# Starting a fused attention and feed-forward kernel on Trainium2: E and F over two queues and cast early, k ahead of half of q, and the q repack moved

## The chip, the cores and the metric

The kernel runs on one core of one Trainium2 chip. The metric is the device time of one execution in microseconds (us). An execution takes about 415 us, and executions of one kernel mostly agree within 0.3% (here four of the kernel before lie from 414.90 to 415.64 us). One of several executions is profiled. The engines are named here as in the profile: PE is TensorE (matmul), PEld its weight loads, DVE is VectorE, ACT is ScalarE, POOL is GpSimd, and SP is SyncE, which here only issues transfers. PSUM is the memory that PE writes its results to; another engine copies them out.

## The reference, cut to what matters

Attention over a projected sequence (E and F shorten k and v from 1024 to 64 rows), followed by a feed-forward layer that takes the maximum of three up-projections:

```python
# q, k, v: (8, 8, 1024, 64); E, F: (64, 1024)
k_proj = np.einsum('ks,bhsd->bhkd', E, k)
v_proj = np.einsum('ks,bhsd->bhkd', F, v)
attn   = softmax(q @ k_proj.transpose(0, 1, 3, 2) / 8)
x      = (attn @ v_proj).transpose(0, 2, 1, 3).reshape(8192, 512)
h      = np.maximum(np.maximum(x @ w1, x @ w2), x @ w3)   # 512 -> 768
out    = h @ w_out                                        # 768 -> 512
```

## The kernel before

The batches are pipelined: while the feed-forward layer of one batch runs, the attention of the next is fitted between its steps. Batch 0 has nothing to hide behind, so its start is a series of small dependent steps. It loads, casts and transposes E, F and q, projects k, computes the scores of its four head pairs (numbered 0 to 3), and projects v. In the names below, T means transposed: kp and vp are k and v projected, kpT is kp transposed, xT is the attention's result, and hT what the down-projections read. `idle(n)` issues n filler matmuls on a constant tile, whose results nobody reads.

```python
def idle(n):
    t, ns = bank()
    for _ in range(n):
        nc.tensor.matmul(out=t, lhsT=warm[:, 0:P], rhs=warm, start=True, stop=True)
    free[ns[0]] = pe(n * MM)

nc.scalar.dma_start(out=ef_f[0:KP], in_=E)          # ScalarE's queue
nc.scalar.dma_start(out=ef_f[KP:P], in_=F)          # behind E
for i in range(2):                                  # SP's queue: q, q, k, k, v
    nc.sync.dma_start(out=q_f[i], in_=view(q, 0)[:, 4 * i:4 * i + 4, 0:SPC])
for i in range(2):
    nc.sync.dma_start(out=k_f[i], in_=view(k, 0)[:, 4 * i:4 * i + 4])
for (a, b), t in zip(v_heads, v_f):
    nc.sync.dma_start(out=t, in_=view(v, 0)[:, a:b])
# ... (cut)
idle(9)
cast_q(0, "v"); cast_q(1, "s")        # "v" VectorE, "s" ScalarE, "g" GpSimd
turn_ef()                             # 8 fp32 transposes on PE, 2 copies
turn_q(0); turn_q(1)
idle(3)
cast_q(2, "v"); cast_q(3, "s")
turn_q(2); turn_q(3)
idle(7)
cast_k(0, 0, "v"); cast_k(0, 1, "s")
kp = k_half(0)                        # first k projection
# ... (cut: scores, exps, second k projection, sums, casts of v)
idle(3)
v_part(0)                             # first v projection
copy("v", v_t[:, 4:6], v_f[1])
for g in (2, 3):
    invert(0, g, *C0, sums(0, g, *C0))
scale_x(0, 0, *C0, values(0, 0, *C0))
idle(2)
copy("v", v_t[:, 6:8], v_f[2])
v_part(1)
scale_x(0, 1, *C0, values(0, 1, *C0))
idle(2)
v_part(2)
scale_x(0, 2, *C0, values(0, 2, *C0))
# then the first up-projection of the feed-forward layer
```

For later batches q is repacked by four VectorE copies and turned by a DMA transpose. The plan says behind which step this stands: steps 0 to 5 are up-projections, 6 to 9 down-projections.

```python
out = {(0, 1): [za(n, 0), sc(n, 1)], (0, 3): [za(n, 1), sc(n, 2)], ...}   # cut
if n + 1 < B:
    out[0, 4] = [qd(n + 1)]           # the repack of q
```

The softmax here doesn't subtract the row's maximum and nothing guards it: scores larger than these inputs give would overflow.

Of the kernel before, what the change touches and what calls it, by code (L numbers as in the profile page):

```python
# [8 lines left out]
FP32 = mybir.dt.float32  # L9
# [6 lines left out]
def kernel(  # L16
# [57 lines left out]
    def two():  # L74
        n = min(range(0, 8, 2), key=lambda n: max(free[n:n + 2]))
        deal((n, n + 1))
        return psum_t[:, n:n + 2, :], (n, n + 1)
# [6 lines left out]
    def pe(dt, wait=0.0):  # L84
        clock["pe"] = max(clock["pe"], wait) + dt
        return clock["pe"]

    def runs(eng, ready, dt, ns=()):
        if eng in clock:
            clock[eng] = max(clock[eng], ready + 0.06) + dt  # L90
            for n in ns:
                free[n] = clock[eng]
            return clock[eng]
        return ready + dt
# [1 line left out]
    MM = 0.216  # L96

    def copy(eng, o, i, ns=(), dt=0.65):
        {  # L99
            "v": nc.vector.tensor_copy, "s": nc.scalar.copy, "g": nc.gpsimd.tensor_copy  # L100
        }[eng](out=o, in_=i)
        runs(eng, clock["pe"] if ns else 0.0, dt, ns)

    def after(dma, earlier):
        tc.add_manual_dep(
# [7 lines left out]
    def view(src, b):  # L113
        return src[b].rearrange("h (p si) d -> p h si d", si=SI)


    ident = const.tile([P, P], BF16, name="ident")
    ident_f = const.tile([P, P], FP32, name="ident_f")
    ones = const.tile([P, HALF], BF16, name="ones")
    warm = const.tile([P, 512], BF16, name="warm")  # L120
    w_sb = [const.tile([P, NCT, DF], BF16, name=f"w{i}_sb") for i in range(3)]
# [16 lines left out]
    first = first_ctx.enter_context(tc.tile_pool(name="first", bufs=1))  # L138

    ef_f = first.tile([P, S], FP32, name="ef_f")  # L140
    q_f = [first.tile([P, 4, SPC, D], FP32, name=f"q_f{i}") for i in range(2)]
    k_f = [first.tile([P, 4, SI, D], FP32, name=f"k_f{i}") for i in range(2)]
    q_c = [first.tile([P, 2, SPC, 2, D], BF16, name=f"q_c{i}") for i in range(2)]
    v_heads = [(0, 4), (4, 6), (6, 8)]
    v_f = [first.tile([P, b - a, SI, D], FP32, name=f"v_f{a}") for a, b in v_heads]
    nc.scalar.dma_start(out=ef_f[0:KP], in_=E)
    nc.scalar.dma_start(out=ef_f[KP:P], in_=F)
    for i in range(2):
        nc.sync.dma_start(out=q_f[i], in_=view(q, 0)[:, 4 * i:4 * i + 4, 0:SPC])
    for i in range(2):  # L150
        nc.sync.dma_start(out=k_f[i], in_=view(k, 0)[:, 4 * i:4 * i + 4])
    for (a, b), t in zip(v_heads, v_f):
        nc.sync.dma_start(out=t, in_=view(v, 0)[:, a:b])

# [1 line left out]
    nc.vector.memset(warm, 0.0)  # L156
    make_identity(nc, ident)
    nc.vector.memset(ones, 1.0)
    nc.vector.tensor_copy(out=ident_f, in_=ident)

    def load_w(i, half):
        cts = slice(half * NCT // 2, (half + 1) * NCT // 2)
        w = (moe_w1, moe_w2, moe_w3)[i].rearrange("(ct p) j -> p ct j", p=P)
        nc.gpsimd.dma_start(out=w_sb[i][:, cts, :], in_=w[:, cts, :])

    def load(b):
        tiles = tuple(
# [190 lines left out]
# [5 lines that stand above are left out]
        free[ns[0]] = pe(n * MM)  # L363

    def turn_ef():
        t, ns = two()
        src = ef_f.rearrange("k (p si) -> k p si", si=SI)
        for si in range(SI):
            nc.tensor.transpose(  # L369
                out=t[:, si // 4, (si % 4) * P:(si % 4 + 1) * P], in_=src[:, :, si],  # L370
                identity=ident_f,
            )
        pe(2.0)
        for i in range(2):
            copy(
                "vs"[i], efT[:, 4 * i:4 * i + 4].rearrange("p si t k -> p (si t k)"),
                t[:, i], ns[i:i + 1],
            )

    def cast_q(g, eng):  # L380
        copy(
            eng, q_c[g // 2][:, g % 2].rearrange("p si h d -> p h si d"),
            q_f[g // 2][:, 2 * (g % 2):2 * (g % 2) + 2],
        )

    def turn_q(g):
        t, ns = two()
        t = t.bitcast(BF16)[:, 0]
        for si in range(SPC):
            nc.tensor.transpose(  # L390
                out=t[:, si * P:(si + 1) * P],
                in_=q_c[g // 2][:, g % 2, si].rearrange("p h d -> p (h d)"),
                identity=ident,
            )
        pe(0.3)
        copy(
            "v", qTs[0][:, g * SI:g * SI + SPC, :].rearrange("a si p -> a (si p)"),
            t[:, 0:CHUNK], ns, 0.43,
        )

    def cast_k(i, j, eng):
        copy(eng, k_t[:, 4 * i + 2 * j:4 * i + 2 * j + 2], k_f[i][:, 2 * j:2 * j + 2])

    def k_half(i):
        t, ns = bank()
        proj(0, 1, t, [slice(4 * i + 2 * j, 4 * i + 2 * j + 2) for j in range(2)], 2 * D)
        kp = att.tile([P, 2 * D], BF16, name="kp0")
        copy("v", kp, t[:, 0:2 * D], ns, 0.3)
        return kp

    def k_turn(i, kp):
        t, ns = two()
# [11 lines left out]
        copy("v", vps[0][:, a:b].rearrange("a h d -> a (h d)"), t[:, 0:(b - a) * D], ns, 0.4)  # L424

    C0 = (0, SPC)
    idle(9)
    cast_q(0, "v")
    cast_q(1, "s")
    turn_ef()  # L430
    turn_q(0)
    turn_q(1)
    idle(3)
    cast_q(2, "v")
    cast_q(3, "s")
    turn_q(2)
    turn_q(3)
    idle(7)
    cast_k(0, 0, "v")
    cast_k(0, 1, "s")  # L440
    kp = k_half(0)
    idle(2)
    k_turn(0, kp)
    idle(2)
    sc01 = [scores(0, g, *C0) for g in (0, 1)]
    for g in (0, 1):
        exps(0, g, *C0, sc01[g])
    idle(2)
    cast_k(1, 0, "v")
    cast_k(1, 1, "g")  # L450
    load_w(0, 0)
    load_w(0, 1)
    kp = k_half(1)
    z01 = [sums(0, g, *C0) for g in (0, 1)]
    invert(0, 0, *C0, z01[0])
    k_turn(1, kp)
    idle(2)
    sc23 = [scores(0, g, *C0) for g in (2, 3)]
    exps(0, 2, *C0, sc23[0])
    invert(0, 1, *C0, z01[1])  # L460
    exps(0, 3, *C0, sc23[1])
    copy("v", v_t[:, 0:2], v_f[0][:, 0:2])
    copy("g", v_t[:, 2:4], v_f[0][:, 2:4])
    load_w(1, 0)
    load_w(1, 1)
    load_w(2, 0)
    nc.gpsimd.dma_start(out=q_t[:, :, SPC:], in_=view(q, 0)[:, :, SPC:])
    load_w(2, 1)
    nc.gpsimd.dma_start(out=wout_sb, in_=moe_w_out.rearrange("(jt p) m -> p jt m", p=P))
    idle(3)  # L470
    v_part(0)
    copy("v", v_t[:, 4:6], v_f[1])
    for g in (2, 3):
        invert(0, g, *C0, sums(0, g, *C0))
    scale_x(0, 0, *C0, values(0, 0, *C0))
    idle(2)
    copy("v", v_t[:, 6:8], v_f[2])
    v_part(1)
    scale_x(0, 1, *C0, values(0, 1, *C0))
    idle(2)  # L480
    v_part(2)
    scale_x(0, 2, *C0, values(0, 2, *C0))
    first_ctx.close()


# [101 lines left out]
    def plan(b):  # L587
        n = b + 1
        if b == 0:
            c1 = (SPC, SPC)  # L590
            return {
                (0, 5): [za(0, 0, *c1), sc(0, 2, *c1)],
                (0, 6): [za(0, 1, *c1), sc(0, 3, *c1)],
                (0, 7): [za(0, 2, *c1)],
                (0, 8): [za(0, 3, *c1), ld(1)],
                (0, 9): [kproj(1)],
                (1, 0): [kt(1), qp(1, (0,)), qp(1, (1,))],
                (1, 1): [sc(1, 0), qp(1, (2,)), qp(1, (3,))],
                (1, 2): [vproj(1), sc(1, 1), sc(1, 2), ld(2)],
                (1, 3): [za(1, 0), sc(1, 3)],  # L600
                (1, 4): [za(1, 1)],
                (1, 5): [za(1, 2)],
                (1, 7): [za(1, 3)],
            }
        if b == 1:
            return {
                (0, 1): [qd(2)],
                (0, 5): [kproj(2), vproj(2), ld(3)],
                (0, 6): [kt(2)],
                (0, 7): [sc(2, 0)],  # L610
                (0, 9): [za(2, 0), sc(2, 1)],
                (1, 1): [za(2, 1), sc(2, 2)],
                (1, 3): [za(2, 2), sc(2, 3)],
                (1, 5): [za(2, 3)],
            }
        if b == 2:
            return {
                (0, 0): [qd(3)],
                (0, 2): [kproj(3), vproj(3), ld(4)],
                (0, 3): [kt(3)],  # L620
                (0, 4): [sc(3, 0)],
                (0, 6): [za(3, 0), sc(3, 1)],
                (1, 0): [za(3, 1), sc(3, 2), qd(4)],
                (1, 2): [za(3, 2), sc(3, 3), kproj(4), vproj(4), ld(5)],
                (1, 4): [kt(4)],
                (1, 5): [za(3, 3), sc(4, 0)],
            }
        if n == B:
            return {}
        out = {  # L630
            (0, 1): [za(n, 0), sc(n, 1)],
            (0, 3): [za(n, 1), sc(n, 2)],
            (0, 9): [za(n, 2), sc(n, 3)],
            (1, 3): [za(n, 3)],
        }
        if n + 1 < B:
            out[0, 4] = [qd(n + 1)]
            out[0, 9] += [kproj(n + 1), vproj(n + 1)]
            out[1, 1] = [kt(n + 1)]
            out[1, 3] += [sc(n + 1, 0)]  # L640
        if n + 2 < B:
            out[1, 1] += [ld(n + 2)]
        return out
# [56 lines left out]
```

## Time and profile before

| | before |
|---|---|
| time, median of the first 3 executions | 415.45 us (414.9 to 415.64) |
| profiled execution: span | 413.7 us |
| PE busy | 396.6 us (96%) |
| first up-projection matmul | 25.75 us |
| first up-projection result copied out of PSUM | 29.02 us |
| from that copy to the end | 384.7 us |

Lines of the page of the kernel before: its span, its engine table (busy us, share, instructions) and the granted clock in 40 slices of the span, in tenths:

```profile
span 413.7 us, 6017 instructions
...
PE 396.6 (96%) x2397; PEld 181.4 (44%) x2442; DVE 204.4 (49%) x315; ACT 192.4 (47%) x280; POOL 27.7 (7%) x37
...
PEclk9999999999999999999999999999999999999999
...
```

PE is the bound (96% busy), so time is to be had only where PE waits or runs fillers. The next lines are from the timeline of the kernel before: start, duration (of a merged group), engine, line, operation, result and operands, count, and in brackets what ended the idle time before it.

```profile
...
1.20 4.02 PE L362 MATMUL banks<-warm 128*128 128x512 bf16 x9 [1.20 <-DVE warm L156]
...
9.05 1.94 PE L369 MATMUL banks<-ident_f,ef_f 128*128 128x128 f32 x8 [3.83 <-DMA ef_f<-in_F_dram]
...
14.32 0.99 DVE L99 CAST k_t<-k_f_92 128x1024 bf16<-128x1024 f32 x1
...
15.38 0.64 PE L267 MATMUL banks<-k_t,efT 128*64 128x128 bf16 x16
...
19.56 0.41 PE L186 MATMUL banks<-qT,kpT 64*64 64x256 bf16 x8
...
20.66 1.06 PE L267 MATMUL banks<-v_t,efT 128*64 128x256 bf16 x16
...
25.75 13.12 PE L491 MATMUL banks<-xT,w_sb 128*128 128x512 bf16 x59
...
29.02 0.58 ACT L99 COPY hs<-banks 128x512 f32<-128x512 f32 x1 [4.36 <-PE banks L491]
...
```

The reader should see how late everything follows from E and F: they are transposed at 9.05 us, after F's load. k's cast on VectorE begins at 14.32, the k projection at 15.38, the scores of pairs 2 and 3 at 19.56, the v projection at 20.66. The `ACT COPY hs` line is the first result of the up-projection to leave PSUM. Filler matmuls of 512 columns follow each other in 0.43 us at the top (nine in 4.02 us). Later ones take 0.22, like the up-projections at the bottom (59 in 13.12 us). I read this as PE at half and at full clock: in the changed kernel, whose record shows a granted clock of 0.50 from 24.23 to 27.65 us, the up-projections start 0.43 us apart in that stretch and 0.22 behind it, at 1.00. The clock record, which the digits above show, begins at 13.77 us here, and the time before counts in them as full, so they do not show the half clock of the first fillers.

The transfers of E and F in the transfer view of the same kernel (queue, size, us from issue to landing; E is issued at 0.74, F at 1.31):

```profile
...
ef_f<-in_E_dram ACTq DMA_DIRECT2D x1, 256.0 KB, 5.2
ef_f<-in_F_dram ACTq DMA_DIRECT2D x1, 256.0 KB, 7.6
...
```

After 60 us, PE waits for almost nothing. The waits view from 60 us on (us in total, times, longest) has one line that matters:

```profile
...
PE banks L566 <- DVE hT L501: 2.8, 4, 0.9
...
```

One of the places, in the timeline of the kernel before:

```profile
...
291.94 1.42 DVE L99 COPY q_p<-q_t 128x1024 bf16<-128x1024 bf16 x4
...
292.70 1.24 PE L566 MATMUL banks<-wout_sb,hT 128*128 128x512 bf16 x5
...
294.06 0.69 DVE L501 TENSOR_TENSOR hT<-banks,m_2761 128x512 bf16<-128x512 f32 x1
...
294.81 1.90 PE L566 MATMUL banks<-wout_sb,hT 128*128 128x512 bf16 x7 [0.87 <-DVE hT L501]
...
```

VectorE does the q repack (merged here to 1.42 us of busy time, four copies of 0.42) ahead of the maximum that completes hT. The down-projection issues five matmuls and then waits for hT.

### The profile page before, as it was taken

To read this page: it belongs to the slowest core of one execution; us is meant where nothing else is said; L and a number is where in the kernel's file an instruction comes from. 1 tells how busy PE (TensorE), PEld (TensorE's weight loads), DVE (VectorE), ACT (ScalarE), POOL (GpSimd) and SP (SyncE) were. 2 spreads that over 40 slices of the span, in tenths; PEclk is the share of its full clock that TensorE was granted. 3 is DMA by queue.
4 is the path that set the end of the run, shared out by engine and by line. 5 is a ranking of instruction groups with operands and counts; after the bars stand their busy time and mean duration, and the time that the engine had idled before them with its cause. 6 is when DMAs were issued, how large, how long until landed. Compare 5 with 4: busy or idle time off the path is not lost.

```text
span 413.7 us, 6017 instructions
## 1 busy us (share of the span) xinstructions
PE 396.6 (96%) x2397; PEld 181.4 (44%) x2442; DVE 204.4 (49%) x315; ACT 192.4 (47%) x280; POOL 27.7 (7%) x37
## 2 busy tenths in 40 slices
PE   5999999999999999999999999999999999999996
PEld 2544354345444544444444435444354444444442
DVE  1556765564373626636363563525465273525251
ACT  1450617722765266547435546436445466432322
POOL 0620111002000200200200002000000000000000
PEclk9999999999999999999999999999999999999999
DMA  8999879947932699697798119940510202020202
GB/s 246 361 206 201 138 172 173 184 129 128 239 65 102 121 195 246 92 233 133 209 184 163 56 45 222 202 143 0 152 53 2 101 0 103 0 103 0 102 2 101
DMA packets 58332, 54.92 MB, mean 133 GB/s; under 512 B 25920, under 2 KB 51776, under 8 KB 58304
## 3 DMA queue, kind: packets, MB, share of 16 engines
q0 software_dynamic: 25296, 25.69, 39.1%
q1 hardware_dynamic: 32848, 28.31, 20.9%
q10 hardware_dynamic: 160, 0.52, 0.6%
q8 instruction: 19, 0.31, 0.3%
q14 instruction: 9, 0.07, 0.1%
HBM read 57.15 MB, written 16.78 MB: 179 GB/s over the span
## 4 chain that ended last, share of the span: by engine, by line
PE 87%; ACT 4%; DVE 3%; issue 3%; DMA 2%; ACTq 0%; DVEq 0%
PE banks L491 56%; PE banks L566 19%; PE banks L206 4%; PE banks L267 4%; PE banks L186 2%; DMA ef_f<-in_F_dram 2%; PE banks L362 1%; ACT zl L219 1%; ACT zi L225 1%; DVE q_p L99 1%; ACT pT L197 1%; PE banks L278 1%; DVE hT L501 1%; PE banks L369 0%; PE banks L390 0%
## 5 line engine op out<-in xcount | busy, mean ns | idle before, releaser
L491 PE MATMUL banks<-xT,w_sb 128*128 128x512 bf16 x1119 | 253.6, 379 | 2.0 <-issue 0.6
L491 PEld LDWEIGHTS <-w_sb 128*128 128x128 bf16 x1152 | 109.9, 98 | 137.1 <-issue 9.7
L549 ACT COPY h1s<-banks 128x512 f32<-128x512 f32 x90 | 52.4, 582 | 93.0 <-PE banks L491 90.3
L566 PE MATMUL banks<-wout_sb,hT 128*128 128x512 bf16 x375 | 86.6, 379 | 3.5 <-DVE hT L501 2.8
L236 DVE TENSOR_TENSOR xT<-banks,zi 128x1024 bf16<-128x1024 f32 x28 | 34.3, 1224 | 76.3 <-ACT zi L225 55.3
L99 ACT COPY o_sb<-banks 128x512 f32<-128x512 f32 x60 | 35.0, 584 | 56.8 <-PE banks L566 56.8
L566 PEld LDWEIGHTS <-hT 128*128 128x128 bf16 x384 | 36.4, 98 | 49.6 <-DVE hT L501 6.3
L219 ACT ACTIVATE zl<-banks 128x1024 f32<-128x1024 f32 (+1 forms) x36 | 33.5, 930 | 29.5 <-PE banks L206 28.6
L197 ACT ACTIVATE pT<-banks 128x1024 bf16<-128x1024 f32 (+1 forms) x36 | 33.3, 930 | 15.8 <-PE banks L186 15.8
L225 ACT ACTIVATE zi<-zl 128x1024 f32<-128x1024 f32 x28 | 29.6, 1057 | 0.9
L172 POOL DMA_DIRECT2D q_t<-in_q_dram x7 | 6.1, 876 | 208.3 <-DMA qT<-q_p 104.6
L267 PEld LDWEIGHTS <-efT 128*64 128x64 bf16 x304 | 14.3, 110 | 5.3 <-issue 5.3
L206 PE MATMUL banks<-pT,ones 64*64 64x512 bf16 (+1 forms) x144 | 13.8, 375 | 1.1 <-ACT pT L197 0.6
L186 PE MATMUL banks<-qT,kpT 64*64 64x512 bf16 (+1 forms) x144 | 13.5, 359 | 0.9 <-ACT pT L197 0.5
L206 PE MATMUL banks<-pT,vp 64*64 64x512 bf16 (+1 forms) x144 | 13.4, 355 | 0.2 <-DVE vp L99 0.2
L362 PE MATMUL banks<-warm 128*128 128x512 bf16 x31 | 10.9, 478 | 1.7 <-DVE warm L156 1.2
L206 PEld LDWEIGHTS <-ones 64*64 64x64 bf16 x144 | 4.2, 103 | 14.2 <-issue 14.0
L99 DVE CAST vp<-banks 64x256 bf16<-64x256 f32 (+2 forms) x17 | 7.0, 410 | 5.7 <-ACT vp L99 3.5
L267 PE MATMUL banks<-v_t,efT 128*64 128x256 bf16 (+1 forms) x160 | 9.6, 263 | 0.0
L267 PE MATMUL banks<-k_t,efT 128*64 128x256 bf16 (+1 forms) x144 | 8.7, 264 | 0.0
L99 ACT CAST vp<-banks 64x256 bf16<-64x256 f32 x14 | 5.1, 364 | 7.7 <-PE banks L267 7.5
L99 DVE COPY q_p<-q_t 128x1024 bf16<-128x1024 bf16 x24 | 8.5, 419 | 0.0
(252 smaller groups left out, 222.6 us busy)
## 6 DMA issues: line engine op xcount, KB each, us to landing
out_dram<-o_sb SPq DMA_DIRECT2D x30, 512.0 KB, 3.1
k_t<-in_k_dram POOLq DMA_DIRECT2D x7, 1024.0 KB, 14.8
q_t<-in_q_dram POOLq DMA_DIRECT2D x7, 1024.0 KB, 9.6
v_t<-in_v_dram POOLq DMA_DIRECT2D x7, 1024.0 KB, 18.9
w_sb<-in_moe_w_dram POOLq DMA_DIRECT2D x6, 384.0 KB, 8.7
k_f_92<-in_k_dram SPq DMA_DIRECT2D x1, 1024.0 KB, 9.4
k_f_93<-in_k_dram SPq DMA_DIRECT2D x1, 1024.0 KB, 11.3
v_f_96<-in_v_dram SPq DMA_DIRECT2D x1, 1024.0 KB, 13.2
```

Source lines behind the costliest of these rows:

```text
L99: {"v": nc.vector.tensor_copy, "s": nc.scalar.copy, "g": nc.gpsimd.tensor_copy}[eng](out=o, in_=i)
L186: nc.tensor.matmul(out=t[c * HALF:(c + 1) * HALF, hp, 0:n * P], lhsT=kpTs[b][rows, g, :], rhs=qTs[b][rows, at:at + n, :], start=True, stop ...
L197: nc.scalar.activation(out=pTs[b, g, lo], in_=t, func=AF.Exp, scale=scale)
L206: nc.tensor.matmul(out=t[hp * HALF:(hp + 1) * HALF, c, 0:nsi * HALF], lhsT=w(rows, hp), rhs=p[rows, hp, :], start=True, stop=True,)
L219: nc.scalar.activation(out=zl, in_=t, func=AF.Ln)
L225: nc.scalar.activation(out=zi, in_=zl, func=AF.Exp, scale=-1.0)
L236: nc.vector.tensor_tensor(out=xTs[b][:, g, lo:lo + nsi, :].rearrange("a (c s) p -> a c (s p)", c=2), in0=t, in1=zi, op=ALU.mult,)
L267: nc.tensor.matmul(out=t[hh * HALF:(hh + 1) * HALF, 0:width], lhsT=efT[:, si, kv - 1, :], rhs=qkv[b][kv][:, heads[hh], si, :], start=(si = ...
L362: nc.tensor.matmul(out=t, lhsT=warm[:, 0:P], rhs=warm, start=True, stop=True)
L491: nc.tensor.matmul(out=h, lhsT=w_sb[i][:, ct, jt * P:(jt + 1) * P], rhs=xTs[b][:, ct, ch * SPC:(ch + 1) * SPC, :], start=(ct == 0), stop=( ...
L549: nc.scalar.copy(out=h1s, in_=h[0][0])
L566: nc.tensor.matmul(out=o_ps, lhsT=hTs[b, ch][:, jt, tt * P:(tt + 1) * P], rhs=wout_sb[:, jt, :], start=(jt == 0), stop=(jt == NJT - 1),)
```

## The change

Its intent: get E and F earlier by loading them on two queues, and cast them to bf16 so that their transposes are cheaper; start k's chain, which feeds ScalarE's long series of exps, ahead of the second half of q; and move the repack to the down-projection steps, where VectorE has little to do (in the kernel before it is busy for 0.00 of the 5.2 us from 294.80 to 300.00).

```diff
     nc.scalar.dma_start(out=ef_f[0:KP], in_=E)
-    nc.scalar.dma_start(out=ef_f[KP:P], in_=F)
+    nc.sync.dma_start(out=ef_f[KP:P], in_=F)
 ... (cut)
+    load_q(0)
+    load_k(0)
+    load_k(1)
+    load_q(1)
 ... (cut)
     def turn_ef():
+        for i in range(2):
+            cols = slice(i * S // 2, (i + 1) * S // 2)
+            copy("vs"[i], ef_b[:, cols], ef_f[:, cols])
 ... (cut: transposes in bf16 instead of fp32)
-    idle(9)
+    idle(7)
+    turn_ef()
     cast_q(0, "v")
     cast_q(1, "s")
-    turn_ef()
+    idle(3)
     turn_q(0)
     turn_q(1)
 ... (cut: first k projection, scores and exps of pairs 0 and 1, second k projection)
+    load_w(0, 0, k_copy)
+    load_w(0, 1)
+    cast_q(2, "v")
+    cast_q(3, "v")
     idle(2)
+    turn_q(2)
+    sc23 = [scores(0, 2, *C0)]
+    turn_q(3)
+    sc23.append(scores(0, 3, *C0))
 ... (cut)
+    z23 = [sums(0, g, *C0) for g in (2, 3)]
+    for g in (2, 3):
+        invert(0, g, *C0, z23[g - 2])
+    v_part(0)
 ... (cut)
     scale_x(0, 0, *C0, values(0, 0, *C0))
-    idle(2)
-    copy("v", v_t[:, 6:8], v_f[2])
+    scale_x(0, 1, *C0, values(0, 1, *C0))
     v_part(1)
-    scale_x(0, 1, *C0, values(0, 1, *C0))
-    idle(2)
+    copy("v", v_t[:, 6:8], v_f[2])
+    scale_x(0, 2, *C0, values(0, 2, *C0))
     v_part(2)
 ... (cut)
-            out[0, 4] = [qd(n + 1)]
+            out[0, 6] = [qd(n + 1)]
```

## The prediction

(In it, the SWDGE queue is the one that takes the transfers issued on POOL, q0 software_dynamic on the page. In the kernel before it moved nothing from 14 to 17.9 us and 0.08 MB from 17.9 to 18.6, while SP's last load landed at 18.8.)

> **What bounds it.** TensorE: busy 396.6 of 413.7 us, granted clock 0.999 (engine table, cores view). Time can only come from where it waits or runs fillers.
>
> 1. The start. Timeline: the first up-projection matmul is issued at 25.75 us. Before it the chain runs through the load of F (7.6 us, landed 8.9; E landed 5.96, q's first half 6.14), 1.94 us of fp32 transposes of E/F, then q, then k. 31 filler matmuls (10.9 us, groups table) occupy the engine meanwhile. k's first half lands at 11.2 us, but its cast on VectorE starts at 14.32, behind both halves of q; its projection starts at 15.38, v's at 20.66, and 5.1 us of v work follow.
> 2. Three down-projection starts, each waiting 0.87 us for hT from VectorE (waits view: 4 waits, 2.8 us; the fourth is 0.2). Just before (two looked up), VectorE does the q repack: four copies of 0.42 us.
>
> **What changes, costed from the trace.**
>
> - F no longer queues behind E. I expect both at about 5.3 us, not 8.9. (F beside q's second half moves at 210-310 GB/s, later 410.) [...] I don't count on bandwidth, but F now precedes q in its ring. The rest may land 0 to 1 us earlier.
> - Casting E/F to bf16 adds 0.43 us (VectorE) beside 0.62 (ScalarE), and turns 1.94 us of fp32 transposes into about 1 us (eight in bf16: 1.02-1.06).
> - k of batch 0 passes half of q: it lands at 9 to 10, is cast on three engines, and its projection starts at about 10.5 (15.4 before). First exp near 12.3 (17.36 before). 5 us gained there.
> - But much is given back. VectorE then does, in series, kp and kpT copies, k cast (0.7-1.0), kp/kpT again, two q casts (0.43 each), two qT copies, v cast (0.7). v still lands at 15-16 (the same bytes precede it), and sums of head pairs 2 and 3 precede its projection. I get it at 17.5 to 19 (20.66 before). From there to the first up-projection, VectorE's series (0.42+0.69+0.69+0.3+0.69+0.3, with a 0.64 projection) takes 5.2-5.5, about as before. First up-projection at 23.5 (22.5 to 24.7): **2.2 us gained**.
> - Weights: the SWDGE queue is served only once the SP loads are through (dma view by windows: q0 idle until 18), first w half landed 20.6. No bound at 23.5; later halves come each 1.9 us and are used each 2.6 us.
> - The repack moves to where VectorE has finished hT and the down-projection (5.2 us) is copied by ScalarE: the three waits vanish, **2.6 us gained**. The transpose lands 5.6 us after issue, over 10 us before its use.
>
> **Time.** 415.45 - 2.2 - 2.6 = 410.65, rounded to **410.5 us**, 80% range 408.5 to 412.5. Chances: faster by over 2% (below 407.1) 0.05; within 2% 0.94; slower 0.01.
>
> **What would show it.** Timeline: E/F transposes near 6 instead of 9.05; k projection 10.5; v projection 17.5-19; first up-projection 23.5. Waits after 60 us: 0.87 us waits gone. First up-projection to end: 388.0 becomes 385.4.
>
> **What would make it wrong.** E and F landing later (then only 1 us of the start); a VectorE series shorter than I count (4 us gained at the start); a first weight half that lands after 23 us; the moved transposes delaying stores on their queue, or q loads.

## The result, and the profile after

The changed kernel takes 413.85 us (median of 4, 413.14 to 414.4), the kernel before 415.39 in the same rounds. The ratio is 0.9963, with a 95% interval of 0.9944 to 0.9983. A ratio here and below is the mean time of one kernel's fast executions over that of the other's of the same rounds, so it is not quite the ratio of the medians quoted. All executions count as fast. The forecast of 410.5 us (408.5 to 412.5) is missed: 1.5 us gained instead of 4.9.

The same lines of the page of the changed kernel (the third slice of the clock is an 8 now):

```profile
span 411.5 us, 6052 instructions
...
PE 398.6 (97%) x2434; PEld 180.3 (44%) x2434; DVE 205.0 (50%) x315; ACT 192.6 (47%) x280; POOL 29.3 (7%) x39
...
PEclk9989999999999999999999999999999999999999
...
```

The timeline of the changed kernel, with the lines that answer to those of before:

```profile
...
6.55 1.08 PE L382 MATMUL banks<-ident,ef_b 128*128 128x128 bf16 x8 [2.19 <-ACT ef_b L99]
...
9.67 2.13 PE L371 MATMUL banks<-warm 128*128 128x512 bf16 x7
...
10.26 0.92 DVE L99 CAST k_t<-k_f_92 128x1024 bf16<-128x1024 f32 x1
...
11.73 0.64 PE L276 MATMUL banks<-k_t,efT 128*64 128x128 bf16 x16
...
18.44 0.30 PE L195 MATMUL banks<-qT,kpT 64*64 64x256 bf16 x4 [0.52 <-DVE qT L99]
...
19.68 1.06 PE L276 MATMUL banks<-v_t,efT 128*64 128x256 bf16 x16
...
21.33 0.41 PE L215 MATMUL banks<-pT,vp 64*64 64x256 bf16 x8 [0.59 <-DVE vp L99]
...
23.30 0.30 PE L215 MATMUL banks<-pT,vp 64*64 64x256 bf16 x4 [0.99 <-DVE vp L99]
...
23.90 0.80 PE L276 MATMUL banks<-v_t,efT 128*64 128x128 bf16 x16 [0.29 <-DVE v_t L99]
...
25.08 0.43 PE L215 MATMUL banks<-pT,vp 64*64 64x256 bf16 x4 [0.38 <-DVE vp L99]
...
25.44 14.19 PE L503 MATMUL banks<-xT,w_sb 128*128 128x512 bf16 x60
...
29.79 0.59 ACT L99 COPY hs<-banks 128x512 f32<-128x512 f32 x1 [7.62 <-PE banks L503]
...
```

And E and F in its transfer view (both are issued at 0.74):

```profile
...
ef_f<-in_E_dram ACTq DMA_DIRECT2D x1, 256.0 KB, 4.0
ef_f<-in_F_dram SPq DMA_DIRECT2D x1, 256.0 KB, 5.0
...
```

The two timelines side by side. "Lead" is how much earlier the changed kernel is:

| step | before | forecast | after | lead |
|---|---|---|---|---|
| E/F transposes start | 9.05 | near 6 | 6.55 | 2.50 |
| first k projection | 15.38 | 10.5 | 11.73 | 3.65 |
| second k projection | 17.92 | - | 14.40 | 3.52 |
| scores of pair 3 (the last) | 19.70 | - | 18.44 | 1.26 |
| first v projection | 20.66 | 17.5 to 19 | 19.68 | 0.98 |
| first up-projection | 25.75 | 23.5 | 25.44 | 0.31 |
| first up-projection result copied | 29.02 | - | 29.79 | -0.77 |
| from there to the end | 384.73 | 2.6 less | 381.72 | 3.01 |

So the lead of 3.65 us melts step by step and ends as a loss of 0.77 us. The last row alone pays for the whole gain: 3.01 - 0.77 = 2.24 us, which is the difference of the spans (413.7 to 411.5).

The last step from 0.31 to -0.77 is odd: the same matmuls need 3.27 us (25.75 to 29.02) before and 4.35 us after. The record of the granted clock tells why. In the changed kernel it goes to 0.50 at 24.23 us and back to 1.00 at 27.65, 3.41 us later, and the spell at 1.00 before it, from 10.58 to 24.23, is four times as long. The up-projections start 0.43 us apart at 0.50 and 0.22 behind it, at 1.00. The following lines are the windows view cut in such steps of 3.41 us (in the kernel before counted from 13.77, where its record begins): window, its length, then the busy us (and instructions) of PE, PEld, DVE, ACT and POOL, the granted clock, the DMA share and GB/s. First the kernel before:

```profile
...
20.60:24.01 3.41, 3.10 (x51) 1.84 (x52) 2.24 (x5) 3.30 (x6) 2.67 (x3) 1.00 1.16 209
24.01:27.42 3.41, 3.10 (x36) 1.55 (x35) 2.45 (x6) 0.63 (x1) 0.00 (x0) 1.00 1.16 209
...
```

And the changed kernel:

```profile
...
20.82:24.23 3.41, 1.61 (x40) 1.17 (x42) 2.90 (x6) 1.28 (x3) 3.41 (x5) 1.00 1.14 192
24.23:27.65 3.42, 3.04 (x21) 1.20 (x17) 1.20 (x3) 0.00 (x0) 0.91 (x2) 0.50 1.12 190
27.65:31.06 3.41, 3.41 (x18) 1.52 (x17) 0.71 (x2) 1.04 (x2) 0.00 (x0) 1.00 1.34 183
...
```

In the changed kernel PE is busy for 1.61 of 3.41 us between 20.82 and 24.23, and for the next step it gets half the clock (0.50), into the first up-projection. In the kernel before PE is busy for 3.10 of 3.41 us in the like window and keeps its clock (1.00). The waits of 0.59, 0.99 and 0.29 us in the timeline above fill most of the gap (the one of 0.38 falls in the next step). They stand in the v part, which lost five of its seven fillers.

The down-projections lost their waits. The same place as before, in the changed kernel (the repack now comes after hT; the matmuls run through):

```profile
...
291.50 3.19 PE L578 MATMUL banks<-wout_sb,hT 128*128 128x512 bf16 x14
291.70 0.69 DVE L513 TENSOR_TENSOR hT<-banks,m_2748 128x512 bf16<-128x512 f32 x1
292.31 1.42 DVE L99 COPY q_p<-q_t 128x1024 bf16<-128x1024 bf16 x4
...
```

### The profile page after: what moved, and what is told of

It is laid out like the page before. It is cut to its first block, busy times and chain, and to the rows that moved or that the text cites. A ratio compares the mean times of both kernels' runs of the same rounds, so it can differ in the third digit from the quotient of the medians.

```text
span 411.5 us, 6052 instructions
## 1 busy us (share of the span) xinstructions
PE 398.6 (97%) x2434; PEld 180.3 (44%) x2434; DVE 205.0 (50%) x315; ACT 192.6 (47%) x280; POOL 29.3 (7%) x39
## 4 chain that ended last, share of the span: by engine, by line
PE 94%; DVE 2%; ACT 2%; DMA 1%; issue 1%; DVEq 0%; ACTq 0%
PE banks L503 61%; PE banks L578 20%; PE banks L215 4%; PE banks L276 4%; PE banks L195 2%; DMA ef_f<-in_F_dram 1%; PE banks L371 1%; PE banks L287 1%; ACT pT L206 1%; DVE xT L245 0%; PE banks L402 0%; ACT zl L228 0%; ACT o_sb L99 0%; PE banks L382 0%; ACT zi L234 0%
## 5 line engine op out<-in xcount | busy, mean ns | idle before, releaser
L503 PE MATMUL banks<-xT,w_sb 128*128 128x512 bf16 x1152 | 257.5, 380 | 0.0
L371 PE MATMUL banks<-warm 128*128 128x512 bf16 x26 | 9.6, 497 | 1.2 <-DVE warm L164 1.2
```

The costliest lines, as they stand in the source:

```text
L503: nc.tensor.matmul(out=h, lhsT=w_sb[i][:, ct, jt * P:(jt + 1) * P], rhs=xTs[b][:, ct, ch * SPC:(ch + 1) * SPC, :], start=(ct == 0), stop=( ...
```

## The experiments

Sixteen runs were made (e6 and e14 repeat the changed kernel, e13 repeats e3), four at a time, each group on one chip with runs of the kernel before, in five rounds. My theory after reading the traces: the repack move is worth about 3 us, and the new start is a loss, because VectorE's order holds up the v part and because PE's waits there cost it the clock. The rival: the start gains something and the repack gives less than forecast.

### e1: the repack move alone

```diff
 # the kernel before
-            out[0, 4] = [qd(n + 1)]
+            out[0, 6] = [qd(n + 1)]
```

> The kernel before with the q repack moved to the down steps and nothing else. My theory: the repack move is worth its three waits of 0.87 us, 2.6 us, and perhaps 0.3 more, and the rest of the change gives nothing or costs time. So 412.7 us (412.3 to 413.1), about 1 us FASTER than the whole change (413.85). Rival: the repack move gave only part and the start of the kernel gave the rest: then 413.5 to 415.

Measured: 412.11 us (411.08 to 412.67), ratio 0.9929 (0.9912 to 0.9946). That is 1.7 us less than the whole change by the medians, 1.4 by the ratios, and slightly below the expected range. From the first copy out of PSUM to the end its profile has 381.58 us, against 384.73 before. So one line gives more than the whole change does.

### e2: the whole change without the repack move

```diff
 # the changed kernel
-            out[0, 6] = [qd(n + 1)]
+            out[0, 4] = [qd(n + 1)]
```

> The whole change with the repack put back to its old step, so only the new start. My theory: the new start alone is a loss, because the first up-projection copy out of PSUM came 0.77 us later than before (29.79 against 29.02): 416.2 us (415.8 to 416.8), slower than before by 0.8 us or 0.2%. Rival (the start gains some of what I forecast): 413.5 to 415.

Measured: 417.35 us (415.11 to 419.77), ratio 1.0065 (1.0033 to 1.0097). The new start alone is a loss, by more than expected, and its executions scatter over 4.7 us. In the profiled one the clock was at a half for three steps on end, 19.84 to 30.08 us, and the first copy came at 32.31. The rival falls.

### e3, e13 and e14: fillers back into the v part

```diff
 # the changed kernel
+    idle(2)
     scale_x(0, 0, *C0, values(0, 0, *C0))
     scale_x(0, 1, *C0, values(0, 1, *C0))
     v_part(1)
     copy("v", v_t[:, 6:8], v_f[2])
+    idle(4)
     scale_x(0, 2, *C0, values(0, 2, *C0))
+    idle(1)
     v_part(2)
+    idle(1)
```

> The whole change with eight filler matmuls put back into the v part, where TensorE waits 0.59, 0.99, 0.29 and 0.38 us for VectorE. My theory: these waits let the granted clock fall to a half from 24.2 to 27.6 us, which costs 1.1 us in the first up-projection matmuls and about 0.4 us before. With fillers the clock stays at 1.0 in every half microsecond from 20 on, the first up-projection stays within 0.3 us of 25.4 or comes a little earlier, and the time is 412.5 us (412.1 to 413.0). Rival (the lost gain is all in VectorE's series, the clock is of no account): 413.6 to 414.2.

Measured: 412.77 us (412.19 to 414.85), ratio 0.9955 (0.9932 to 0.9978). In the profile the clock stays full from 10.12 us to near the end, the first up-projection comes at 25.47 as in the changed kernel, and the first copy at 28.75 instead of 29.79. The mechanism shows, but one long execution of six (414.85) blurred the ratio, and the changed kernel had been measured on another chip. So both were run again on one chip, as e13 (the same code) and e14 (the changed kernel).

> The same kernel as e3, the whole change with eight fillers in the v part, now on one chip with the whole change (e14). My theory: the clock's drop between 20 and 28 us costs 1.0 us, so 412.7 us, a ratio to before 0.0020 to 0.0035 lower than that of e14. Rival (the drop is compensated, or comes anyway at another place): within 0.0012 of e14.

> The whole change, unaltered, as reference: 413.8 us (413.0 to 414.4), ratio 0.9963 to 0.9972 as in its two runs so far.

Measured: e13 412.53 us (412.19 to 413.35), ratio 0.9939 (0.9923 to 0.9955). e14 414.06 us (413.09 to 417.70), ratio 0.9984 (0.9953 to 1.0014). The medians differ by 1.5 us. The means differ by 0.0045 of the time before, 1.9 us, more than the expected 0.0020 to 0.0035, because of e14's execution of 417.70; the two intervals just touch. That one was profiled. Its windows, cut at the clock's steps, with the same columns as above:

```profile
...
15.76:19.18 3.42, 2.17 (x29) 0.88 (x23) 2.06 (x7) 2.90 (x5) 2.62 (x4) 1.00 0.99 329
19.18:22.59 3.41, 2.95 (x27) 1.66 (x30) 1.14 (x2) 2.00 (x5) 3.41 (x5) 0.50 1.14 197
22.59:26.00 3.41, 1.62 (x34) 0.90 (x31) 2.48 (x5) 1.09 (x2) 3.30 (x4) 1.00 1.12 179
26.00:29.42 3.42, 2.24 (x22) 1.39 (x23) 1.99 (x4) 0.00 (x0) 0.00 (x0) 0.50 1.13 192
29.42:32.83 3.41, 3.41 (x9) 1.22 (x8) 0.00 (x0) 0.00 (x0) 0.00 (x0) 0.50 1.34 194
...
```

The clock fell after a window with PE busy for 2.17 of 3.41 us, came back, fell again after one with 1.62, and then stayed low for a second step, after a window at half clock with PE busy for 2.24. In e13, in the same part of the start (the second window holds the first up-projections):

```profile
...
22.54:25.95 3.41, 3.15 (x49) 1.61 (x42) 2.98 (x6) 0.63 (x1) 3.41 (x5) 1.00 1.13 178
25.95:29.37 3.42, 3.37 (x19) 1.59 (x20) 0.69 (x1) 0.00 (x0) 0.20 (x1) 1.00 1.15 190
...
```

Eight fillers of 0.22 us, which compute nothing, make the kernel 1.5 us faster by the medians. In the first pair of profiles the up-projection starts at the same time and its first result is out 1.04 us earlier (28.75 against 29.79), so it is the clock that they save.

### e4: the v part in another order

```diff
 # the changed kernel
+    copy("v", v_t[:, 6:8], v_f[2])
     z23 = [sums(0, g, *C0) for g in (2, 3)]
 ... (cut)
     v_part(0)
 ... (cut)
-    scale_x(0, 0, *C0, values(0, 0, *C0))
-    scale_x(0, 1, *C0, values(0, 1, *C0))
     v_part(1)
-    copy("v", v_t[:, 6:8], v_f[2])
-    scale_x(0, 2, *C0, values(0, 2, *C0))
     v_part(2)
+    scale_x(0, 0, *C0, values(0, 0, *C0))
+    scale_x(0, 1, *C0, values(0, 1, *C0))
+    scale_x(0, 2, *C0, values(0, 2, *C0))
```

> The whole change with the three v projections put next to each other, the last v cast taken ahead of them and the three scalings after them; the work is the same. It tests that VectorE's order in the v part (scalings ahead of the last cast and of the vp copies) held the end of the start back. If so: first up-projection at 23.0 to 23.8 instead of 25.44, no wait over 0.5 us in the v part, the clock stays at 1.0 as a side effect, and the time is 410.3 us (409.8 to 411.5). Rival (something else, such as weights or the exp chain, holds the up-projection at 25.4): within 0.5 us of 413.8, with a wait of the first up-projection for it.

Measured: 410.42 us (410.03 to 410.72), ratio 0.9890 (0.9871 to 0.9908). With the same work in another order on VectorE, 3.4 us come off the changed kernel's 413.85 by the medians, 3.0 by the ratios. The first up-projection comes at 23.24, as expected (25.44 in the changed kernel). The expected side effect on the clock did not come true: it was at half from 18.40 to 21.81, now under the v projections, after a window over the late half of q (14.99 to 18.40) with PE busy for 0.61 of it. In its timeline:

```profile
...
18.69 3.45 PE L276 MATMUL banks<-v_t,efT 128*64 128x256 bf16 x48
...
```

### e5: the kernel before without its fillers in the v part (a miss)

```diff
 # the kernel before
-    idle(3)
     v_part(0)
 ... (cut)
-    idle(2)
     copy("v", v_t[:, 6:8], v_f[2])
     v_part(1)
 ... (cut)
-    idle(2)
     v_part(2)
```

> The kernel before with the seven filler matmuls of its v part taken out, nothing else. The converse of the filler experiment. My theory: TensorE then waits in pieces between 19.9 and 25 us, the granted clock falls to a half for some 3.4 us in most executions, and the time rises by 1 to 3 us to 416.5-418.5, with a wider spread than the 1.7 us of before. Rival (fillers are idle work, without them the start can only be shorter): 414.8 to 415.4.

Measured: 414.59 us (414.12 to 415.92), ratio 0.9996 (0.9981 to 1.0011). The rival was right: removing fillers does not lose the clock by itself. The windows of e5, cut at its clock's steps, show what PE did:

```profile
...
18.34:21.75 3.41, 2.41 (x39) 1.29 (x39) 1.99 (x4) 3.35 (x7) 3.41 (x5) 1.00 1.16 210
21.75:25.17 3.42, 2.59 (x54) 1.80 (x48) 3.23 (x8) 2.13 (x4) 0.68 (x1) 1.00 1.16 208
...
```

The old order of the v part keeps PE busy for 2.4 to 2.6 of 3.41 us without any filler, and the clock stays. So the loss in the changed kernel takes both: the order that makes PE wait (with the old one, e5 keeps 1.00), and the missing fillers (with eight, e13 keeps 1.00).

### e6: the whole change once more

> The whole change, unaltered, as the reference on the same chip for the two kernels that follow: 413.8 us, with executions from 413 to 415.

Measured: 413.80 us (413.06 to 413.97), ratio 0.9968 (0.9956 to 0.9980). As before. The three sets of the changed kernel hold 15 executions, none of them with a full clock. The seven with a mean granted clock of 0.994 take 413.5 us on average, the six with 0.990 or 0.991 take 414.1. One step at half clock lowers the mean by half of 3.41/412, 0.004. This is a correlation: the record has some drops in the first waits as well, where they cost less, and the mean counts the time before the first record as full.

### e7: e4 with fillers also in q's part

```diff
 # e4
-    idle(2)
+    idle(4)
     turn_q(2)
+    idle(2)
     sc23 = [scores(0, 2, *C0)]
     turn_q(3)
+    idle(2)
     sc23.append(scores(0, 3, *C0))
```

> The reordered v part (e4) with six more filler matmuls in the stretch from 15 to 18 us, where TensorE waits 0.29, 0.52 and 0.52 us for VectorE to cast and copy q. In e4 the clock was at 0.55 to 0.60 from 18 to 22 us and the v projections took 3.45 us instead of 2.3. My theory: the fillers keep the clock at 1.0, the v projections take 2.3 us, and the time falls by about 1 us against e4's 410.4, to 409.4 us (408.9 to 410.0). Rival (fillers delay the q copies as much as they save): 410.3 or more.

Measured: 410.04 us (409.49 to 410.67), ratio 0.9882 (0.9868 to 0.9896). The clock holds there and the v projections take 1.96 us (2.3 expected):

```profile
...
20.27 1.96 PE L276 MATMUL banks<-v_t,efT 128*64 128x256 bf16 x48
...
```

But the time falls by only 0.0008 of the time before, 0.3 us, with overlapping intervals, and not to the expected 409.4. From the v projection to the first up-projection it takes 3.05 us (20.27 to 23.32), against 5.76 in the changed kernel. In the profiled execution k came late: its first projection stood at 12.33 us against 10.32 in e4, as the clock was at a half from 8.49 to 11.90 (the seven fillers ahead of it took 2.84 us, in e4 1.67). How the early part falls on the clock's steps differs from execution to execution.

### e8: the late half of q cast earlier (no gain)

```diff
 # e7
+    cast_q(2, "v")
+    cast_q(3, "s")
     idle(3)
     kp, k_copy = k_half(1)
+    turn_q(2)
 ... (cut: the old casts and turn_q(2) behind k_turn(1) removed, turn_q(3) moved ahead of the scores, four fillers fewer)
```

> e7 with the second q half cast earlier (one pair on VectorE ahead of the k copies, one on ScalarE) and its first transpose directly behind the second k projection. It tests that the serial steps of the late q half (cast, transpose, copy, scores, twice) ate most of the lead that k had won: 3.5 us at the second k projection, 1.3 us at the last scores of the whole change. If so the last scores come 1 us earlier than in e7 and the time falls by 0.5 to 1 us, to 408.4-409.0. Rival (v's landing or the weights now bound): within 0.3 us of e7.

Measured: 410.04 us (408.93 to 410.86), ratio 0.9880 (0.9862 to 0.9898), the same as e7. From the second k projection to the last scores it took 3.14 us (15.51 to 18.65) instead of 4.04 in e7. But the sums behind them then waited 0.35 and 0.18 us for ScalarE's exps, and the v projection came at 20.56 (20.27 in e7). So the serial steps of the late q half do hold up the scores, as I thought; but most of their gain is lost at the next engine.

### e9: E and F in fp32

```diff
 # e7: turn_ef as in the kernel before, without the cast
-        for i in range(2):
-            cols = slice(i * S // 2, (i + 1) * S // 2)
-            copy("vs"[i], ef_b[:, cols], ef_f[:, cols])
 ... (cut: eight transposes of ef_f with ident_f)
```

> e7 (reordered v part, fillers kept dense) with E and F transposed in fp32 as before, so without the bf16 cast; two queues stay. From F's landing to the last efT copy it took 2.7 us before and 2.9 us after, so the cast saves no latency by my reading. My theory: within 0.4 us of e7's 410.0, ratio to before 0.987 to 0.989. Rival (cheaper transposes are worth their saving of about 1 us): 411 or more, ratio 0.990 to 0.991.

Measured: 410.01 us (409.62 to 410.98), ratio 0.9878 (0.9861 to 0.9894). The cast to bf16 is worth nothing: the transposes get cheaper (1.12 us for the eight in fp32 here, 0.71 in bf16 in e7), but a cast of 0.43 us (VectorE) and 0.62 (ScalarE) stands ahead of them.

### e10: F behind E again

```diff
 # e7
-    nc.sync.dma_start(out=ef_f[KP:P], in_=F)
+    nc.scalar.dma_start(out=ef_f[KP:P], in_=F)
```

> e7 with F back behind E on the ScalarE queue. F then lands near 8.9 instead of 5.8 us and E/F are transposed near 9.7. My theory: the first k projection comes 1.5 to 2.5 us later and all of it reaches the end of the start, as q, k and v then wait for VectorE behind it: 411.8 us (411.0 to 412.6), ratio 0.991 to 0.994. Rival (v's landing bounds the start, k's lead is spare): within 0.5 us of e7, ratio below 0.9895.

Measured: 413.27 us (412.40 to 413.94), ratio 0.9953 (0.9938 to 0.9969) against 0.9882: 0.0071 of the time before, 2.9 us lost, more than expected. E and F are transposed at 9.02 us, and the first k projection comes at 15.02. In this execution PE had nothing at all to do from 4.46 to 7.87, a whole step of the clock, and then had half the clock until 14.70 (the fillers from 12.14 to 14.28 start 0.43 us apart). So F's late landing costs its wait, and in this execution the clock behind it too. The runs do not separate the two shares.

### e11: the loads of q ahead of those of k again

```diff
 # e7
     load_q(0)
+    load_q(1)
     load_k(0)
     load_k(1)
-    load_q(1)
```

> e7 with the loads in the old order, both q halves ahead of k; the order of work stays. k's first half then lands about 1.3 us later (the time of 0.5 MB at 400 GB/s). My theory: the first k projection moves by 0.5 to 1 us only, because the seven fillers before it end 0.6 to 1.2 us after the k cast, and the time by as much: 410.3 to 411.0, ratio 0.989 to 0.990. Rival (loading order is what gives the gain): 411.3 or more.

(The 400 GB/s is what the changed kernel moved during its loads: 404, 399 and 409 in the three steps from 7.17 to 17.41 us.)

Measured: 410.79 us (410.50 to 410.94), ratio 0.9894 (0.9879 to 0.9910), 0.5 us above e7 by the ratios, on the expected side, though the intervals overlap.

### e12: fewer fillers ahead of the first k projection

```diff
 # e7
-    idle(7)
+    idle(4)
     cast_k(0, 0, 2, "v")
```

> e7 with four instead of seven fillers ahead of the first k projection. In e7 they run at half clock, take 2.84 us and end 1.0 us after the last k cast. My theory: the first k projection comes 0.6 to 1.0 us earlier and the time falls by 0.3 to 0.9 us to 409.1-409.7 (ratio 0.986 to 0.9875), unless the clock, with fewer fillers, warms one step of 3.4 us later. Rival (v's landing bounds): 409.9 to 410.3.

Measured: 409.84 us (409.60 to 410.48), ratio 0.9874 (0.9859 to 0.9889). In the profile the first k projection comes at 11.22 us instead of 12.33 and the first copy out of PSUM at 25.95 instead of 26.92. In the ratios only 0.3 us of this is left, within the intervals. Inconclusive as to time.

### e15 and e16: two lines of the change in the old kernel, and a version that beats both

With F's queue found to be worth 2.9 us (e10), it was open whether k ahead of q and the new order are needed at all.

```diff
 # e15: the kernel before
-    nc.scalar.dma_start(out=ef_f[KP:P], in_=F)
+    nc.sync.dma_start(out=ef_f[KP:P], in_=F)
 ... (cut)
-            out[0, 4] = [qd(n + 1)]
+            out[0, 6] = [qd(n + 1)]
```

> The kernel before with two lines changed: F on the SP queue, and the repack moved. E and F stay in fp32, k stays behind q, the work keeps its order and fillers. My theory: F landing 3 us earlier moves the whole old start ahead until k's landing at 11.2 us holds it, so the first k projection comes at 12.5 to 13.5 instead of 15.4 and the first up-projection at 23 to 24; 410.0 us (409.3 to 411.0), ratio 0.986 to 0.990, better than the whole change by 3 to 4 us. Rival (k ahead of q and the new order are needed to use F's lead): 411.4 to 412.3, as with the repack move alone.

Measured: 410.35 us (409.64 to 411.14), ratio 0.9884 (0.9862 to 0.9905). Two lines give 4.9 us, where the whole change gave 1.5. In its timeline:

```profile
...
5.94 1.12 PE L369 MATMUL banks<-ident_f,ef_f 128*128 128x128 f32 x8 [0.73 <-DMA ef_f<-in_F_dram]
...
12.27 0.95 PE L267 MATMUL banks<-k_t,efT 128*64 128x128 bf16 x16 [0.65 <-DVE k_t L99]
...
18.82 1.06 PE L267 MATMUL banks<-v_t,efT 128*64 128x256 bf16 x16 [0.33 <-DVE v_t L99]
...
23.78 9.46 PE L491 MATMUL banks<-xT,w_sb 128*128 128x512 bf16 x42
```

The first k projection is later than in the changed kernel (12.27 against 11.73), but the v projection is earlier (18.82 against 19.68) and the first up-projection much earlier (23.78 against 25.44), with a full clock from 5.82 us on. At full clock the eight fp32 transposes take 1.12 us, not 1.94.

```diff
 # e16: e15
     idle(3)
-    v_part(0)
     copy("v", v_t[:, 4:6], v_f[1])
+    copy("v", v_t[:, 6:8], v_f[2])
+    v_part(0)
     for g in (2, 3):
         invert(0, g, *C0, sums(0, g, *C0))
-    scale_x(0, 0, *C0, values(0, 0, *C0))
-    idle(2)
-    copy("v", v_t[:, 6:8], v_f[2])
     v_part(1)
-    scale_x(0, 1, *C0, values(0, 1, *C0))
-    idle(2)
     v_part(2)
+    scale_x(0, 0, *C0, values(0, 0, *C0))
+    scale_x(0, 1, *C0, values(0, 1, *C0))
     scale_x(0, 2, *C0, values(0, 2, *C0))
```

> e15 with the last two v casts taken ahead of the v projections and the projections put closer together. If VectorE's order in the v part binds here too, 0.5 to 1.5 us below e15; if v's landing (16 to 19 us) or the exp chain of ScalarE binds, within 0.4 us of e15.

Measured: 408.66 us (408.04 to 410.05), ratio 0.9848 (0.9827 to 0.9868), the best, 1.5 us below e15 by the ratios, as expected if VectorE's order binds here too: 6.6 us under the 415.27 of the kernel before in its rounds, and 5.4 under the 414.06 of e14 on the same chip.

## Why the prediction was wrong

Point by point, as the prediction put it:

1. **"The three waits vanish, 2.6 us gained"**: the mechanism was right and the size was short. From the first copy out of PSUM to the end there are 384.7 us (before and e5) and 385.1 (e2) in the three profiles with the old place and 381.6 to 381.9 in all fifteen profiles with the new one: about 3.0 us. The term that was mis-sized is the wait itself. Its 0.87 us begins where the profile says the matmul before it ended, but such ends are modelled and overlap with the next matmul's start: in the record each of these matmuls lasts 0.38 us, and they start 0.216 us apart. In the timeline of before, five start from 292.70 on, so the sixth was due at 293.78 and started at 294.81: 1.03 us lost. Three times this is 3.1.
2. **"Both [E and F] at about 5.3 us, not 8.9"**: close. F landed at 5.79 (0.74 + 5.0, in rounded lines), E at 4.7. I did not count on more bandwidth from a second queue, and none shows: the last load of v landed at 18.8 us before (issue at 7.17 and 11.6 us) and 19.1 after (9.53 and 9.6). The gain is, by my reading, one of order: F stands ahead of q on SP's queue and no longer behind E on ScalarE's, and q's first half, now behind it, lands at 7.00 instead of 6.15. A run with F on SP's queue behind q, which would show it, was not made. e10 puts this one line at 2.9 us, e15 against e1 at 1.9 us (0.9929 - 0.9884, on two chips).
3. **"Its projection starts at about 10.5"**: 11.73. The last k cast ended at 11.18. Seven fillers ahead of the projection, issued partly at half clock (0.43 us apart up to 10.53, 0.22 after), took 2.13 us and ended later; by the 0.216 us between starts, seven at full clock would take an estimated 1.5. The prediction does not name them. With four (e12 against e7) the projection comes 1.1 us earlier.
4. **"I get it [the v projection] at 17.5 to 19"**: 19.68. An up-projection at 23.5 and a series of 5.2 to 5.5 put it at 18.0 to 18.3, so it was 1.4 to 1.7 us late, of which 1.2 were there at the k projection (point 3). The lead of 3.5 us at the second k projection was down to 1.3 at the last scores, because the late half of q there passes from VectorE to PE and back, twice. I had named this series and counted it a little short. e8 shows that shortening it alone is not enough.
5. **"VectorE's series ... takes 5.2-5.5, about as before", so "First up-projection at 23.5 ...: 2.2 us gained"**: this is the step that failed. The up-projection came at 25.44, only 0.31 us earlier than before, and its first result 0.77 us later. The length of the series was nearly right: 5.76 us, 0.3 to 0.6 more than counted. Wrong was the way of costing this path, by VectorE's durations alone: I had read the order off the diff and added them up, but had not asked what PE would do in the waits, nor seen that most of the fillers were gone, nor that the order could be shorter. e4 shows what the order costs: with the last cast ahead and the scalings behind, the kernel is 3.0 (ratios) to 3.4 us (medians) faster.
6. **The clock**, which the prediction read as 0.999 and took for a constant. The waits of point 5 cost PE half its clock for one step of 3.41 us or more, over the first up-projection. e13 against e14 puts this at 1.5 us by medians, a bit under half of the miss of 3.4 us (413.85 against 410.5). Nothing in the prediction allowed for it.

The sum: the prediction had 2.2 us gained at the start. In the profile it was 0.77 us lost, with 1.08 us (4.35 - 3.27) in the first up-projection alone. The 3.0 us between forecast and profile are thus 1.4 to 1.7 of a late v projection, 0.3 to 0.6 of a longer series, and 1.1 of half clock. The repack gave 0.4 us more than forecast.

The clock can be read more closely. In the 18 traces its record shows 1.00 and 0.50, and every complete spell at 0.50 lasts one, two or three times 3.41 us, at a different phase in each execution: one in the changed kernel (24.23 to 27.65 us) and e4 (18.40 to 21.81), two in e14 (26.00 to 32.83), three in e2 (19.84 to 30.08). I cut the first 36 us of all 18 traces at these steps and took PE's busy share in each from the records of the matmuls (before the first recorded step I took the clock as half, since fillers there are 0.43 us apart). Of the windows at full clock, the 13 that were followed by half had busy shares of 0.00 (e10, 4.46 to 7.87) to 0.635 (e14, 15.76 to 19.18). Of the 111 followed by full, 109 had 0.637 or more, and two had 0.517 (e4, from 4.75) and 0.627 (e6, from 18.19). Of those at half clock, the 31 followed by full had 0.789 or more (e7, from 1.66) and the 18 followed by half 0.75 or less (the changed kernel, from 0.34). In the fatal window of the changed kernel (0.47) the longest single wait was 0.99 us, so here a window was followed by half clock without being idle. These are counts of traces; what the hardware counts, and what share another kernel would need, they do not show.

What stays open: whether F's gain lies in its place ahead of q or in the second queue as such; how much of e10's 2.9 us is F's wait and how much the clock; and what k ahead of q would be worth in a start whose every window is dense (e11 finds 0.5 us for the order of loads alone, within the intervals).

## What to carry to other kernels

Follow a lead to the first instruction of the stage that bounds the kernel, and one step further: it can be won early and be gone at the next engine, so a cost forecast has to state at each step who waits next. Where PE's stretches of work have waits, look at PE's busy share between the steps of its clock before and after a change (here 3.10 and 1.61 of 3.41 us); filler matmuls that look like waste may be what holds the clock, and a better order may do without them. Try the small parts of a change alone: here two of its lines gave three times the gain of the whole.
